# Head of a Fourier-mixing and routed-expert kernel: the second batch's first stage by way of DRAM

## The chip, the cores and the metric

The kernel runs on one core of a Trainium2 chip. The metric is the device time of one execution in microseconds (us). An engine executes its own instructions strictly in the order in which the program gave them to it, so an instruction that waits holds back everything behind it on that engine. PE is TensorE (matmuls and transposes), DVE VectorE, ACT ScalarE, POOL GpSimd, SP SyncE, which here only starts transfers. ACT and POOL start transfers too, in line with their other work.

## The reference, cut to what matters

```python
x: (8, 2496, 256) f32; filt_r, filt_i: (1249, 256); token_ids: (19968,)
w1: (8, 256, 1024); w2: (8, 1024, 256)

X = np.fft.rfft(x, axis=1)
y = np.fft.irfft(X * (filt_r + 1j * filt_i)[None], n=2496, axis=1)
x = y.reshape(19968, 256)
expert = token_ids * 2654435761 % 8
for e in range(8):
    h = np.maximum(x[expert == e] @ w1[e], 0)
    out[expert == e] = h @ w2[e]
```

## The kernel before, in words

**Mixing, per batch.** The transform over 2496 = 39 x 64 positions is done as two nested small transforms, each a matmul against a table, all in fp32. Stage 1 (table `wf_t`) makes 20 complex bins of the 39-point transform for each of 64 sequences. Stage 2 takes two bins at a time: `forward` multiplies by the table `d_t`, DVE multiplies the result in PSUM by the filter (`y`, two halves `z`, and their sum: four instructions), and `back_c` or `back` multiplies by the table `e_t`. Stage 3 (table `wi_t`) ends the inverse transform. Stage 1 and stage 3 are cut into six pieces u of four columns (the last has two), stage 2 into ten pieces.

**Two ways between the stages.** Between stages 1 and 2, and between 2 and 3, the partition axis changes. Batches 2 to 7 do that through DRAM: `stage1` stores to `d1`, `load2` reads it back, `back` stores to `d2`, `load4` reads. Batches 0 and 1 (`first` and `second`) stay on chip: `stage1_c` leaves channels on partitions in `mixed`, `turn2` transposes them for stage 2 with PE and a copy by ACT, `back_c` leaves channels on partitions again in `self.out`, and `turn4` transposes for stage 3 (copies by ACT for batch 0, by DVE for batch 1).

**Scatter and tiles.** `stage3` writes the rows and the number of each token into a buffer `o` (the number by one small DVE instruction, L401; the rows by ACT copies, L259 and L254), and POOL scatters each column with an indirect DMA (L414) into the list `xs`, sorted by expert. One batch has 22 such scatters. Then come 80 expert tiles of 256 tokens (`step`, later `late_step`). Tiles of a stage hold tokens of certain batches only: the first ones those of batches 0 and 1, so their rows (`load`, L807) are fetched when the 44th scatter has landed. The remaining batches are mixed between the tiles' matmuls.

**The head** is everything ahead of the first tile. Its order is a hand-written list `todo` of pairs (t, piece), sorted by t; t is only an order. The order of before: stage 1 of `first`; then a chain of twenty steps for both batches with stage 1 of `second` between them; `turn4` and `stage3` of `first` from the eighth chain step on; then those of `second`; stage 1 of batch 2 between and behind them; `begin`, `load` of tiles 0 and 1. `way_back` makes `e_t` on chip from `d_t` in five pieces. `weights(i, which)` starts the weight transfers of tile i, on ACT's queue for the first two tiles. `begin` opens the tiles' memory pools where the routing pool, the second pair of `o` buffers (`o2`) and others lay, and makes the sums of the first tile's weights (`weight_sums`, L840) on DVE; those of the second follow on POOL.

**Memory that is used twice.** `wts` is both the weights of two tiles and, earlier, input rows and batch 0's `out`. `mid` holds the first batch's `mixed` in rows 0 to 4 and later the slots `t2` and `t1`; the second's data lie in rows 5 to 9.

Of the kernel before, what the change touches and what calls it, by code (L numbers as in the profile page):

```python
# [11 lines left out]
F32 = mybir.dt.float32  # L12
I32 = mybir.dt.int32
# [6 lines left out]
P = 128  # L20
# [14 lines left out]
SG = 4  # L35
# [65 lines left out]
            d.transpose(1, 0, 2, 3, 4).reshape(P, NS, P).astype(f32))  # L101


def route_table():


    t = np.zeros((P, 2 * G + 1 + NQP + HN + 1), np.float32)
    p = np.arange(P)
    r = np.arange(NR)
    t[:NR, G + 1 + NQP:G + 1 + NQP + HN + 1] = (N2 * (r % N1) + np.array(H0)[r // N1])[:, None] + np.arange(HN + 1)  # L110
    for g, b in enumerate(STAGES):
        t[:, g] = p < b * S // NJ
        t[:, G + 1 + NQP + HN + 1 + g] = t[:, g] - (t[:, g - 1] if g else 0)
    t[:, G] = sum(stage_tiles(), []) + [NT] * (P - NT)
    t[:, G + 1:G + 1 + NQP] = p[:, None] * NQP + np.arange(NQP)
    return t
# [3 lines left out]
def kernel(  # L120
# [12 lines left out]
    wf_dram = nc.inline_tensor(wf_host, name="wf_tbl")  # L133
    wi_dram = nc.inline_tensor(wi_host, name="wi_tbl")
    d_dram = nc.inline_tensor(d_host, name="d_tbl")
    r_dram = nc.inline_tensor(route_table(), name="r_tbl")

    xs = nc.dram_tensor("xs", (NT * TB, W), F32)
# [73 lines left out]
    class Batch:  # L212


        def __init__(self, b):
            self.b = b
            self.d1 = self.d2 = None
            self.x, self.t2, self.t4, self.p = {}, {}, {}, {}
            self.g = None
            if b < 2:  # L220

                own = mid[:, 5 * b:5 * b + 5, :].rearrange("p k f -> p (k f)")
                self.mixed = own.rearrange("p (h n s) -> p h n s", h=2, s=NS)
                after = (held[:, 0:NS * C] if b == 0 else mid[:, 0:5, :].rearrange("p k f -> p (k f)"))
                self.out = after.rearrange("p (h n s) -> p h n s", h=2, s=NS)

        def load1(self, v):

            k = self.b * NV + v if self.b < 2 else NV + NV * (self.b > 2) + v
            if k <= NV:  # L230
                xt = wts[0:NR, k, :].rearrange("p (j c) -> p j c", c=C)
            else:
                xt = xpool.tile([NR, XL, C], F32, name=f"x_{self.b}_{v}", tag="x")
            self.x[v] = xt

            n = min(XL, HN + 1 - XL * v)
            for h in range(H):

                (nc.scalar if self.b == 0 and h == 1 else nc.sync).dma_start(out=xt[h:NR:H, 0:n, :],
                                  in_=bass.AP(tensor=x.tensor, offset=x.offset + (self.b * S + H0[h] + XL * v) * C,  # L240
                                              ap=[[N2 * C, N1], [C, n], [1, C]]))
# [28 lines left out]
        def stage1(self, u):  # L270
            if self.d1 is None:
                self.d1 = dpool.tile([N2, 2 * NS, C], F32, name=f"d1_{self.b}", tag="d1")
            v, half = divmod(u, XL // XG)
            sl = slice(half * XG, half * XG + XG)
            if half == 0:
                self.t1 = slot("t1")
            self.products(wf_t, (NR, NR), 2 * NS, self.x[v][:, sl, :], self.t1[:, sl, :], nc.scalar.copy, u, "pa")
            if half == 1:


                moves = self.parts(self.d1, self.t1, v)
                if self.b == 2 and v > 0:
                    put_off.extend(moves)
                    return
                for dram, chip in moves:
                    nc.scalar.dma_start(out=dram, in_=chip)
# [9 lines left out]
        def forward(self, u):  # L296
            ps = fps.tile([P, 2, C], F32, name=f"pb_{self.b}_{u}", tag="f")
            for i in range(2):
                s = 2 * u + i
                rhs = self.t2[u][:, i, :] if self.b < 2 else self.t2[s // SG][:, s % SG, :]  # L300
                nc.tensor.matmul(out=ps[:, i, :], lhsT=d_t[:, s, :], rhs=rhs, start=True, stop=True)  # L301


# [32 lines left out]
        def stage1_c(self, u):  # L336
# [2 lines left out]
            cols = 2 * NS * (H * n if XG * u + n <= HN else H * (n - 1) + 1)  # L339
            c0 = XG * u * 2 * NS * H  # L340
            for h in range(2):
                ps, tag = (fps, "f") if self.b == 0 else (banks["ad"[h]], "ad"[h])
                ps = ps.tile([P, 4, P], F32, name=f"pa_{self.b}_{u}_{h}", tag=tag)
                flat = ps[:].rearrange("p a b -> p (a b)")
                for i in range(n):
                    a = 2 * NS * H * i
# [25 lines left out]
        def turn4(self, u):  # L372
# [2 lines left out]
                self.t4[v] = t4pool.tile([NK, XL, C], F32, name=f"t4_{self.b}_{v}", tag="t4")  # L375
            copy = nc.vector.tensor_copy if self.b else nc.scalar.copy
            for k in range(0, min(XG, HN + 1 - XG * u), 2):
                ps = banks["ad"[k // 2]].tile([P, 2, C], F32, name=f"pu_{self.b}_{u}_{k}", tag="ad"[k // 2])
                rows = [2 * NS * (H if XG * u + k + i < HN else 1) for i in range(2)]
                for i in range(2):  # L380
                    n0 = 2 * H * (XG * u + k + i)
# [15 lines left out]
        def stage3(self, u):  # L397

            n = min(XG, HN + 1 - XG * u)
            o = (o2pool if self.b < 2 and u % 2 else opool).tile([NR, XG, W], F32, name=f"o_{self.b}_{u}", tag="o")  # L400
            nc.vector.tensor_scalar(o[:, 0:n, C:].bitcast(I32),  # L401
                                    tokno[:, XG * u:XG * u + n].unsqueeze(2).to_broadcast([NR, n, W - C]),
                                    float(self.b * S), None, op0=OP.add)
            v, half = divmod(u, XL // XG)
# [22 lines left out]
    def weights(i, which):  # L427
# [2 lines left out]
            return  # L430
        if i >= 2 and which == 0:
            ws[i] = ws[i - 2][0:2]
        eng, kw = nc.scalar if i < 2 else nc.sync, {}
        if which == 0:
            ws[i].append(eng.value_load(chunk_i[0:1, 0, i:i + 1], min_val=0, max_val=E - 1))
            if i >= 2:
# [16 lines left out]

    rctx = ctx.enter_context(ExitStack())
    rpool = pool(rctx, "route", 1)
    o2pool = pool(rctx, "o2", 2)
    nc.sync.dma_start(out=wf_t[:], in_=wf_dram.ap())
    tok_h = dataclasses.replace(moe_token_ids.tensor, shape=list(moe_token_ids.tensor.shape))
    tok = rpool.tile([P, NJ, 2], I32)
# [265 lines left out]
    def chain(k):  # L725

        for step, j in ((Batch.turn2, k + 1), (Batch.back_c, k - 2), (Batch.forward, k)):
            if 0 <= j < NS:
                step(batches[j // (NS // 2)], j % (NS // 2))


    def warm(n):

# [1 line left out]
        for k in range(n):  # L735
            nc.tensor.matmul(out=ps[:, k % 4, :], lhsT=ident[:], rhs=ident[:], start=True, stop=True)

    todo = [(-165, lambda: warm(14))]
    todo += [(t, lambda k=k: load_tables(k)) for k, t in enumerate((-160, -159, -157, -156))]
    todo += [(t, lambda v=v: second.load1(v)) for v, t in enumerate((-159.5, -156.5, -156.4))]  # L740
    todo += [(t, lambda u=u: first.stage1_c(u)) for u, t in enumerate(spaced(-155, -151, NU))]
    todo += [(-154.2, count), (-152, route), (-150.9, later)]
    todo += [(-137.2, places), (-128, tile_experts), (-121, experts), (-90, blanks)]
    todo += [(t, lambda k=k: pads(k)) for k, t in enumerate((10.9, 11.6, 11.9, 16.9, 17.6, 17.95, 22.9))]
    todo += [(t, lambda k=k: spread_filters(k)) for k, t in enumerate((-150.45, -146.6, -143, -137.6))]
    todo += [(t, lambda k=k: way_back(k)) for k, t in enumerate((-150.44, -146.5, -141.8, -137.5, -133.8))]
    todo += [(-150.4, lambda: first.turn2(0))]
    todo += [(t, lambda k=k: chain(k)) for k, t in enumerate(spaced(-150, -105, NS + 2))]
    todo += [(t, lambda u=u: second.stage1_c(u)) for u, t in enumerate(spaced(-147.5, -132, NU))]
    for bt, at in ((first, spaced(-123.7, -105, NU)), (second, spaced(-103, -85, NU))):  # L750
        todo += [(t - 2.6, lambda bt=bt, u=u: bt.turn4(u)) for u, t in enumerate(at)]
        todo += [(t, lambda bt=bt, u=u: bt.stage3(u)) for u, t in enumerate(at)]
    todo += [(-135, lambda: nc.sync.dma_start(out=wi_t[:], in_=wi_dram.ap()))]
    todo += [(t, lambda v=v: batches[2].load1(v)) for v, t in enumerate((-119, -117.5, -116))]
    todo += [(t, lambda u=u: batches[2].stage1(u)) for u, t in enumerate((-101.5, -99.5, -84.8, -84.7, -84.6, -84.5))]

    todo += [(-75.5, lambda: [nc.sync.dma_start(out=dram, in_=chip) for dram, chip in put_off])]
    todo += [(t, lambda k=k: weights(k // 2, k % 2)) for k, t in enumerate((-101, -98, -95, -92))]
    todo += [(-84.9, lambda: begin()), (-84.4, lambda: [load(i) for i in range(2)])]

    def batch(b, t1, t2, t3):

# [5 lines left out]
            out += part1(b, a1, [max(x0, a1[2 * v] - 2.5) for v in range(NV)])  # L768
        return out

    todo += [(-75 + .1 * g, lambda g=g: batches[2].load2(g)) for g in range(4)]
    todo += [(-74.5 + .1 * v, lambda v=v: batches[3].load1(v)) for v in range(2)]
    todo += part2(2, spaced(1, 3.5, N_2), [None] * 4 + [1.5], .6)
    todo += part3(2, spaced(4.6, 7.5, NU), [4.0, 4.1, 4.8]) + part1(3, spaced(1, 4, NU), [None, None, 2])
    todo += part2(3, spaced(6.4, 10, N_2), [5.2, 5.4, 5.6, 6.5, 7.5], .6)
# [15 lines left out]
    def begin():  # L791
        nonlocal gath, work, outs, nums, tpool
        rctx.close()
        tpool, nums, gath = pool(ctx, "tp", 2), pool(ctx, "nums", 8), pool(ctx, "gath", 2)
        outs, work = pool(ctx, "outs", 2), pool(ctx, "work", 1)
        weight_sums(0, nc.vector)

# [36 lines left out]
    def weight_sums(i, eng=None):  # L834

        eng, w1, h = eng or nc.gpsimd, ws[i][0], F // 2
        b11, b12, b21, b22 = [w1[:, d, f * h:f * h + h] for d in range(DP) for f in range(2)]
        t = [tpool.tile([P, h], F32, name=f"tw_{i}_{k}", tag=f"tw{k}") for k in range(4)]
        for k, (p, q) in enumerate(((b12, b11), (b22, t[0][:]), (b22, b12), (b21, t[1][:]))):
            eng.tensor_tensor(t[k][:], p, q, op=OP.subtract)  # L840
        sums[i] = t
# [252 lines left out]
```

## Time and profile before

| | us |
|---|---|
| median of 3 runs | 1433.88 (1428.81 to 1435.61) |
| the profiled execution | 1467.31 |
| its span | 1465.5 |
| first scatter (POOL L414) starts | 74.27 |
| the 44th scatter of the head starts | 144.71 |
| first matmul of the first tile (L850) | 153.56 |

All times on the trace's axis are from the start of the span of the profiled execution. The head is the part before 153.56 us. A row of the timeline has the start, the duration, the engine, the line and the names, and in brackets the idle time ahead of it and what ended it. A row of the windows has, for each engine, busy us and the number of instructions, then PE's granted clock, the share of the DMA engines and GB/s.

### The profile page before, as it was taken

The numbers are of one execution on the slowest core, as the hardware profiler recorded it, in microseconds if no ns is written. First come the engines' busy times: TensorE is split into PE (matmuls) and PEld (weight loads), VectorE is DVE, ScalarE is ACT, GpSimd is POOL, SyncE is SP. The second block draws the span as 40 slices with busy tenths as digits, with TensorE's granted clock in tenths as the row PEclk, the third lists the DMA queues.
The fourth block names the chain that finished last, engine by engine and source line by source line (L and its number), as shares of the span: only waits on it lengthen the run. The fifth ranks groups of instructions, "written<-read, shape, count | busy, mean of one in ns | idle before, by whom it ended". The sixth has DMA issues, their size and how long they took to land.

```text
span 1465.5 us, 26476 instructions
## 1 busy us (share of the span) xinstructions
PE 1397.5 (95%) x9494; PEld 1296.0 (88%) x9494; DVE 877.6 (60%) x1641; ACT 419.1 (29%) x770; POOL 822.0 (56%) x732
## 2 busy tenths in 40 slices
PE   8988799899999989999999999999999999999997
PEld 8876688788988878888999899998999999999997
DVE  7862565366465546533666367744557767677765
ACT  4543122223223212322222222222222222222222
POOL 5065332763475464558435387878955555555553
PEclk9998799999999999999999999999999999999999
DMA  8236775767887597797764777688661616161611
GB/s 231 77 101 214 184 218 158 207 200 238 261 258 252 154 295 234 221 281 227 229 199 139 202 215 235 201 244 247 194 216 44 210 44 208 44 215 45 212 45 34
DMA packets 240947, 272.32 MB, mean 186 GB/s; under 512 B 124940, under 2 KB 210879, under 8 KB 231389
## 3 DMA queue, kind: packets, MB, share of 16 engines
q1 hardware_dynamic: 89087, 169.76, 37.3%
q10 hardware_dynamic: 131806, 56.23, 15.8%
q0 software_dynamic: 19920, 44.59, 8.7%
q8 instruction: 78, 1.28, 0.4%
q14 instruction: 56, 0.46, 0.1%
HBM read 290.24 MB, written 83.53 MB: 255 GB/s over the span
## 4 chain that ended last, share of the span: by engine, by line
PE 78%; DMA 10%; DVE 4%; issue 3%; another core or an unknown queue 1%; POOL 1%; ACTq 1%; ACT 1%; SPq 0%; POOLq 0%; DVEq 0%
PE dps L885 18%; PE up_b L850 8%; PE up_a L850 5%; PE up_c L850 5%; PE pd L257 4%; PE pb L301 4%; PE dnc L912 4%; PE dnb L912 4%; PE dna L912 4%; PE upc L907 4%; PE upa L907 4%; PE pc L324 3%; PE pa L257 2%; DMA t<-d 2%; PE upe L907 2%
## 5 line engine op out<-in xcount | busy, mean ns | idle before, releaser
L885 PE MATMUL dps<-wts,ht 128*128 128x256 f32 x1600 | 367.8, 380 | 1.3 <-ACT ht L854 1.3
L885 PEld LDWEIGHTS dps<-wts,ht 128*128 128x128 f32 x1600 | 302.5, 190 | 45.1 <-ACT ht L854 1.9
L977 POOL DMA_INDIRECT out_dram<-osb,no x158 | 165.1, 1045 | 228.3 <-DVE osb L919 142.8
L414 POOL DMA_INDIRECT xs<-o,sidx x176 | 176.1, 1000 | 197.0 <-ACT o L259 73.4
L840 POOL TENSOR_TENSOR tw<-wts 128x512 f32<-128x512 f32 x158 | 204.3, 1293 | 112.9 <-DMA wts<-in_moe_w_dram 86.2
L840 POOL TENSOR_TENSOR tw<-wts,tw 128x512 f32<-128x512 f32 x158 | 205.1, 1298 | 6.2
L857 DVE TENSOR_TENSOR ht<-up_b,ht 128x512 f32<-128x512 f32 x150 | 103.7, 691 | 141.6 <-PE up_b L850 79.9
L854 ACT ACTIVATE ht<-ht 128x512 f32<-128x512 f32 x150 | 94.3, 630 | 205.7 <-DVE ht L857 172.7
L850 PE MATMUL up_a<-xt,wts 128*128 128x128 f32 x800 | 118.8, 283 | 22.4 <-ACT ht L861 12.8
L850 PEld LDWEIGHTS up_a<-xt,wts 128*128 128x128 f32 x800 | 108.7, 198 | 26.8 <-ACT ht L861 14.1
L311 DVE TENSOR_TENSOR z<-pb,filt 64x512 f32<-64x512 f32 x160 | 110.2, 689 | 36.8 <-PE pc L324 33.4
L890 DVE COPY osb<-dps 128x512 f32<-128x512 f32 x50 | 34.6, 692 | 161.0 <-PE dps L885 112.0
L850 PE MATMUL up_b<-st,tw 128*128 128x128 f32 x800 | 110.9, 284 | 5.8 <-DVE ht L857 4.6
L850 PEld LDWEIGHTS up_b<-st,tw 128*128 128x128 f32 x800 | 101.5, 199 | 7.8 <-issue 7.5
L857 DVE TENSOR_TENSOR ht<-up_c,ht 128x512 f32<-128x512 f32 x100 | 69.0, 690 | 42.9 <-PE up_c L850 29.7
L916 ACT ACTIVATE ht<-ht 128x512 f32<-128x512 f32 x90 | 56.8, 631 | 120.6 <-DVE ht L919 75.2
L257 PE MATMUL pd<-t,wi_t 120*117 120x256 f32 x320 | 79.1, 390 | 7.8 <-DVE t L387 4.0
L327 ACT COPY mid<-pc 128x512 f32<-128x512 f32 x60 | 35.0, 583 | 151.5 <-PE pc L324 94.6
L307 DVE TENSOR_TENSOR y<-pb,filt 128x512 f32<-128x512 f32 x80 | 55.2, 690 | 37.7 <-PE pb L301 25.0
L861 ACT COPY ht<-up_a 128x512 f32<-128x512 f32 x50 | 29.3, 586 | 165.3 <-PE up_a L850 98.2
L257 PEld LDWEIGHTS pd<-t,wi_t 120*117 120x117 f32 x320 | 58.1, 186 | 20.4 <-issue 4.2
L259 ACT COPY o<-pd 117x512 f32<-117x512 f32 x80 | 44.4, 585 | 107.5 <-PE pd L257 40.3
(210 smaller groups left out, 2507.6 us busy)
## 6 DMA issues: line engine op xcount, KB each, us to landing
wts<-in_moe_w_dram SPq DMA_DIRECT2D x160, 1024.0 KB
xg<-xs ACTq DMA_DIRECT2D x321, 64.0 KB
mid<-d SPq DMA_DIRECT2D x60, 256.0 KB
d<-mid ACTq DMA_DIRECT2D x60, 256.0 KB
d_t<-t2s SPq DMA_DIRECT2D x15, 1024.0 KB
e_t<-t2s SPq DMA_DIRECT2D x15, 1024.0 KB
t<-d SPq DMA_DIRECT2D x12, 960.0 KB
x<-in_x_dram SPq DMA_DIRECT2D x36, 312.0 KB
```

The costliest lines, as they stand in the source:

```text
L257: nc.tensor.matmul(out=ps[0:cols * H, k, :], lhsT=w[:], rhs=src[:, 2 * i + k, :], start=True, stop=True)
L301: nc.tensor.matmul(out=ps[:, i, :], lhsT=d_t[:, s, :], rhs=rhs, start=True, stop=True)
L311: nc.vector.tensor_tensor(out=z[b], in0=ps[a], in1=f_t[1][64 * hi:64 * hi + 64, s1:s1 + 2, :], op=OP.mult)
L414: st = nc.gpsimd.indirect_dma_start(out=xs[:], out_offset=bass.IndirectOffsetOnAxis(ap=index, axis=0), in_=rows, in_offset=None, bounds_ch ...
L840: eng.tensor_tensor(t[k][:], p, q, op=OP.subtract)
L850: nc.tensor.matmul(out=ps[bank][:, f, :], lhsT=w[:, f * P:(f + 1) * P], rhs=xx, start=first and f == 0, stop=True, skip_group_check=True)
L854: nc.scalar.activation(out=out, in_=in_, func=AF.Relu)
L857: nc.vector.tensor_tensor(out, ps[bank][:], other, op=OP.add)
L885: nc.tensor.matmul(out=ps[:, h, :], lhsT=ht[:, h, fp, :], rhs=w2[:, fp, :], start=(fp == 0), stop=(fp == FP - 1))
L907: nc.tensor.matmul(out=ps[:, f, :], lhsT=w[:, f * P:(f + 1) * P], rhs=xx, start=first and f == 0, stop=True, skip_group_check=True)
L912: nc.tensor.matmul(out=ps[:, 0, :], lhsT=a[:, f, :], rhs=b[:, f, :], start=first and f == 0, stop=True, skip_group_check=True)
L977: st = nc.gpsimd.indirect_dma_start(out=out[:], out_offset=bass.IndirectOffsetOnAxis(ap=to_rows[i][:, h:h + 1], axis=0), in_=o[:, h, :], i ...
```

## The change

- `second` runs `stage1` (through `d1` in DRAM and `load2`) in place of `stage1_c` and `turn2`; its stages 2 and 3 stay on chip, `out` now in rows 5 to 9 of `mid`.
- `way_back` makes 8 of the 20 parts of `e_t`; the other 12 come from a new DRAM table `e_tbl` by an SP transfer.
- Batch 2 gets a third input buffer (`x2`) and no longer uses a row of `wts`; its stage-1 results go to rows 0 to 3 of `mid`.
- The first two tiles' weights are started by SP.
- The token-number instruction of `stage3` goes to POOL for batches 0 and 1; `turn4` of batch 1 takes the PSUM banks b and c for its odd pieces, a and d for the even ones.
- The two buffers of the weight sums become two pools of one buffer each.
- The head's order list is written anew.

```diff
+def back_table(d):
+    e = d.transpose(2, 1, 0).copy()
+    e[0:64] *= -1
+    return e[:, 8:].copy()
...
+    e_dram = nc.inline_tensor(back_table(d_host), name="e_tbl")
...
-                own = mid[:, 5 * b:5 * b + 5, :].rearrange("p k f -> p (k f)")
-                self.mixed = own.rearrange("p (h n s) -> p h n s", h=2, s=NS)
-                after = (held[:, 0:NS * C] if b == 0 else mid[:, 0:5, :].rearrange("p k f -> p (k f)"))
+                if b == 0:
+                    own = mid[:, 0:5, :].rearrange("p k f -> p (k f)")
+                    self.mixed = own.rearrange("p (h n s) -> p h n s", h=2, s=NS)
+                after = (held[:, 0:NS * C] if b == 0 else mid[:, 5:10, :].rearrange("p k f -> p (k f)"))
...
-            if k <= NV:
+            if self.b == 2 and v == 2:
+                xt = x2pool.tile([NR, XL, C], F32, name="x_2_2", tag="x")
+            elif k <= NV and self.b < 2:
...
-                self.t1 = slot("t1")
+                self.t1 = (slot("t1") if self.b != 2 else
+                           mid[0:NK, 2 * (v % 2):2 * (v % 2) + 2, :].rearrange("p k (j c) -> p (k j) c", c=C))
...
-                rhs = self.t2[u][:, i, :] if self.b < 2 else self.t2[s // SG][:, s % SG, :]
+                rhs = self.t2[u][:, i, :] if self.b == 0 else self.t2[s // SG][:, s % SG, :]
...
-                ps, tag = (fps, "f") if self.b == 0 else (banks["ad"[h]], "ad"[h])
-                ps = ps.tile([P, 4, P], F32, name=f"pa_{self.b}_{u}_{h}", tag=tag)
+                ps = fps.tile([P, 4, P], F32, name=f"pa_{self.b}_{u}_{h}", tag="f")
...
-                ps = banks["ad"[k // 2]].tile([P, 2, C], F32, name=f"pu_{self.b}_{u}_{k}", tag="ad"[k // 2])
+                tag = ("bc" if self.b and u % 2 else "ad")[k // 2]
+                ps = banks[tag].tile([P, 2, C], F32, name=f"pu_{self.b}_{u}_{k}", tag=tag)
...
-            nc.vector.tensor_scalar(o[:, 0:n, C:].bitcast(I32),
+            (nc.gpsimd if self.b < 2 else nc.vector).tensor_scalar(o[:, 0:n, C:].bitcast(I32),
...
-        eng, kw = nc.scalar if i < 2 else nc.sync, {}
+        eng, kw = nc.sync, {}
...
-    o2pool = pool(rctx, "o2", 2)
+    o2pool, x2pool = pool(rctx, "o2", 2), pool(rctx, "x2", 1)
...
-            if 0 <= j < NS:
-                step(batches[j // (NS // 2)], j % (NS // 2))
+            if 0 <= j < N_2:
+                step(first, j)
...
+    head += [(t, lambda u=u: first.stage1_c(u)) for u, t in enumerate(spaced(10, 14, NU))]
...
+    head += [(t, lambda k=k: spread_filters(k)) for k, t in enumerate((22.8, 29, 35.3, 44.8))]
+    head += [(t, lambda k=k: way_back(k)) for k, t in enumerate((22.9, 29.1))]
+    head += [(22.95, lambda: first.turn2(0))]
+    head += [(23 + 3.6 * k, lambda k=k: chain(k)) for k in range(N_2 + 2)]
+    head += [(30, lambda: nc.sync.dma_start(out=e_t[:, 8:, :], in_=e_dram.ap()))]
+    head += [(30.1, lambda: nc.sync.dma_start(out=wi_t[:], in_=wi_dram.ap()))]
+    head += [(t, lambda u=u: second.stage1(u)) for u, t in enumerate((27, 32, 38, 41, 45, 48.5))]
+    head += [(41.5, places), (64, tile_experts), (70, experts), (118, blanks)]
+    head += [(t, lambda g=g: second.load2(g)) for g, t in enumerate((54, 54.1, 54.2, 54.3, 70))]
+    head += [(61 + 2.9 * u, lambda u=u: second.forward(u)) for u in range(N_2)]
+    head += [(61 + 2.9 * (u + 2) - .1, lambda u=u: second.back_c(u)) for u in range(N_2)]
+    at = (64, 69, 74, 79.5, 85, 90)
+    head += [(t, lambda u=u: first.turn4(u)) for u, t in enumerate(at)]
+    head += [(t + 3, lambda u=u: first.stage3(u)) for u, t in enumerate(at)]
+    head += [(t, lambda v=v: third.load1(v)) for v, t in enumerate((72, 73, 74))]
+    head += [(t, lambda k=k: weights(k // 2, k % 2)) for k, t in enumerate((95, 95.1, 95.2, 95.3))]
+    head += [(96 + 5 * u - 4 * (u > 0), lambda u=u: second.turn4(u)) for u in range(NU)]
+    head += [(98 + 5 * u, lambda u=u: second.stage3(u)) for u in range(NU)]
+    head += [(99 + 5 * u - 3 * (u == 5), lambda u=u: third.stage1(u)) for u in range(NU)]
+    head += [(123.5, lambda: begin()), (123.6, lambda: [load(i) for i in range(2)])]
+    head += [(124, lambda: [nc.sync.dma_start(out=dram, in_=chip) for dram, chip in put_off])]
...
+    todo = [(t - 200, piece) for t, piece in head]
...
-        tpool, nums, gath = pool(ctx, "tp", 2), pool(ctx, "nums", 8), pool(ctx, "gath", 2)
+        tpool, nums, gath = [pool(ctx, f"tp{k}", 1) for k in range(2)], pool(ctx, "nums", 8), pool(ctx, "gath", 2)
...
-        t = [tpool.tile([P, h], F32, name=f"tw_{i}_{k}", tag=f"tw{k}") for k in range(4)]
+        t = [tpool[i % 2].tile([P, h], F32, name=f"tw_{i}_{k}", tag=f"tw{k}") for k in range(4)]
```

More of the change, by code (lines that the diff above doesn't have):

```diff
@@ L736, in warm @@
             nc.tensor.matmul(out=ps[:, k % 4, :], lhsT=ident[:], rhs=ident[:], start=True, stop=True)
[L738 to L743, printed above, removed]
@@ L744 @@
-    todo += [(t, lambda k=k: pads(k)) for k, t in enumerate((10.9, 11.6, 11.9, 16.9, 17.6, 17.95, 22.9))]
[L745 to L755, printed above, removed]
@@ L757 @@
-    todo += [(-75.5, lambda: [nc.sync.dma_start(out=dram, in_=chip) for dram, chip in put_off])]
-    todo += [(t, lambda k=k: weights(k // 2, k % 2)) for k, t in enumerate((-101, -98, -95, -92))]
-    todo += [(-84.9, lambda: begin()), (-84.4, lambda: [load(i) for i in range(2)])]
+    third = batches[2]
+    head = [(0, lambda: warm(14))]
+    head += [(t, lambda k=k: load_tables(k)) for k, t in enumerate((5, 6, 8, 9))]
+    head += [(t, lambda v=v: second.load1(v)) for v, t in enumerate((5.5, 8.5, 8.6))]
@@ new lines @@
+    head += [(t, lambda u=u: first.stage1_c(u)) for u, t in enumerate(spaced(10, 14, NU))]
+    head += [(10.8, count), (13, route), (14.1, later)]
+    head += [(t, lambda k=k: spread_filters(k)) for k, t in enumerate((22.8, 29, 35.3, 44.8))]
[3 more added lines that the diff above has]
+    head += [(30, lambda: nc.sync.dma_start(out=e_t[:, 8:, :], in_=e_dram.ap()))]
@@ new lines @@
+    head += [(99 + 5 * u - 3 * (u == 5), lambda u=u: third.stage1(u)) for u in range(NU)]
+    head += [(123.5, lambda: begin()), (123.6, lambda: [load(i) for i in range(2)])]
+    head += [(124, lambda: [nc.sync.dma_start(out=dram, in_=chip) for dram, chip in put_off])]
+    head += [(125 + .1 * g, lambda g=g: third.load2(g)) for g in range(4)]
+    head += [(125.5 + .1 * v, lambda v=v: batches[3].load1(v)) for v in range(2)]
+    todo = [(t - 200, piece) for t, piece in head]
+    todo += [(t, lambda k=k: pads(k)) for k, t in enumerate((10.9, 11.6, 11.9, 16.9, 17.6, 17.95, 22.9))]
@@ L769, in batch @@
         return out
-    todo += [(-75 + .1 * g, lambda g=g: batches[2].load2(g)) for g in range(4)]
-    todo += [(-74.5 + .1 * v, lambda v=v: batches[3].load1(v)) for v in range(2)]
     todo += part2(2, spaced(1, 3.5, N_2), [None] * 4 + [1.5], .6)
```

## The prediction, written before the changed kernel was seen

> **What bounds the kernel now.** I read the page first, then the busy time by stretches of the head, the list of waits from 55 us on, and last the timeline around the longest waits. The page says that the span is PE's.
>
> ```profile
> PE 1397.5 (95%) x9494; PEld 1296.0 (88%) x9494; DVE 877.6 (60%) x1641; ACT 419.1 (29%) x770; POOL 822.0 (56%) x732
> ```
>
> That holds for the tiles, which the change leaves alone. Only the head can get shorter, and it has four stretches with limits of their own, then a gap ahead of the first tile.
>
> ```profile
> 0.00:24.00 24.00, 20.09 (x132) 19.79 (x132) 15.92 (x59) 8.44 (x15) 8.10 (x22) 0.93 0.84 222
> 24.00:64.00 40.00, 37.16 (x266) 35.03 (x266) 35.01 (x48) 21.78 (x38) 13.88 (x13) 1.00 0.44 110
> 64.00:102.40 38.40, 36.60 (x235) 32.29 (x235) 30.37 (x62) 22.70 (x40) 16.75 (x17) 1.00 0.38 118
> 102.40:145.60 43.20, 34.00 (x140) 25.22 (x140) 10.04 (x28) 13.89 (x27) 27.17 (x28) 0.80 0.63 197
> 145.60:153.60 8.00, 0.04 (x1) 0.04 (x1) 6.34 (x6) 0.00 (x0) 6.26 (x5) 0.61 0.61 114
> ```
>
> The reader is to see: input transfers in the first; PE and DVE nearly full in the second; PE (36.6 of 38.4) in the third; no engine full in the fourth, at a granted clock of 0.80; PE idle in the last. The end of the fourth is POOL's last scatter, and how POOL got there is in the waits and the timeline:
>
> ```profile
> POOL xs L414 <- DVE o L401: 14.6, 2, 14.2
> ...
> DVE tw L840 <- DMA xs<-o,sidx: 10.5, 1, 10.5
> ...
> 74.27 1.09 POOL L414 DMA_INDIRECT xs<-o,sidx  x1 [14.25 <-DVE o L401]
> ...
> 96.88 0.99 POOL L414 DMA_INDIRECT xs<-o,sidx  x1 [5.09 <-ACT mid L370]
> ...
> 124.34 5.77 ACTq L445 DMA_DIRECT2D wts<-in_moe_w_dram  x2
> ...
> 128.46 0.99 POOL L414 DMA_INDIRECT xs<-o,sidx  x1 [0.30 <-issue]
> 130.29 0.58 ACT L259 COPY o<-pd 117x512 f32<-117x512 f32 x1 [6.97 <-DMA xs<-o,sidx]
> 131.17 0.99 POOL L414 DMA_INDIRECT xs<-o,sidx  x1 [1.72 <-issue]
> ...
> 144.71 0.90 POOL L414 DMA_INDIRECT xs<-o,sidx  x1 [0.30 <-issue]
> ...
> 152.81 0.70 DVE L818 STREAM_TRANSPOSE xt<-xg 128x512 f32<-128x512 f32 x1
> ```
>
> A scatter costs POOL 0.99 us and 0.30 ahead of it. 44 x 1.29 = 56.8 us, but 74.27 to 145.61 is 71.3, so POOL stood for 14.6 us. The largest pieces: 4.8 at 91.8, about 2.2 each near 110 and 117, about 4 from 128.5 to 135.7. The last has a plain cause: ACT's copies into `o` stood behind a weight transfer that took ACT's queue 5.77 us to start.
>
> **The change part by part.** Every duration is from the profiled execution (1467.31 us; the median run, 1433.88, is 0.977 of it).
>
> *Start, 0 to 24 us:* the same pieces in the same order; nothing.
>
> *24 to 63 us.* PE: a piece of `stage1` is 8 instructions in 1.73 us, of `stage1_c` 16 in 1.78; equal. Three `way_back` pieces go, 0.44 us of PE and 0.69 of ACT each. DVE ends this stretch (the tenth filter product ends at 63.8); its work is the same, but `places` moves forward and can fill DVE's hole of 1.33 us before 48.64, so the products end at 62.5. Against that, `stage1` takes two of the four shared PSUM buffers that `stage1_c` left alone, so PE may wait for DVE; I book the two at 0 to +2. The new table transfer is 0.79 MB on SP behind all input; at the 242 to 247 GB/s of 25 to 40 us it takes 3.1 us, and since the DMA engines are 0.97 busy until 40 and 0.31 after, it lands near 45. Its first user, `back_c`(4), ran at 46.7: hidden, by a margin of 2 us; if late, PE pays it.
>
> *The round trip.* The last `stage1` piece ends on ACT near 54. The nearest row for a store that is read again is `slots`: POOL waited 1.8 us behind its issue. Store 0.64 MB: 2.6 + 1.8; load of the first group, 0.52 MB: 2.1 + 1.8; together 8.3, landing at 62.3. The Trainium skill ("DMA: Bandwidth & Descriptors", Anatomy of one DMA) gives 2.0 us per transfer plus bytes over 436 GB/s, warning of long completion when DRAM is written: 3.5 + 3.2 = 6.7, landing at 60.7. The row is dearer, and I take it. Either way the cover is DVE's backlog until 62.5. `load2` has to wait too for the last `turn2`, near 55, which reads the same rows of `mid`.
>
> *The middle.* Ten `turn2` of `second` go: 10 x 0.64 = 6.4 us of PE, 10 x 0.59 of ACT. PE's work from the second's first `forward` to the first's last `stage3`: 10 x (0.87 + 0.89) + 4.8 (`turn4`) + 9.6 (`stage3`) + 0.3 = 32.3, so 63 to about 96; DVE needs 10 x 2.85 + 2.4 = 31, close behind. In the order list 5.3 us of PE work stand between the first `forward` and `stage3`(0), then 1.7 until ACT has half an `o`: first scatter at 70.5 in place of 74.27. Before, that half was ready at 70.8, and POOL waited for L401 behind DVE's products.
>
> *L401 on POOL.* 12 instructions of 117 x 16 join POOL's own chain. POOL runs none before. The GpSimd rows of like size are 0.20 (copy of one element), 0.29 (128 x 128 select); on DVE it took 0.17. The skill ("GPSIMD Engine Reference", Engine selection) speaks against the move: elementwise work belongs on VectorE, with GpSimd about twice as slow on two inputs and near line rate on one. Twice 0.17 is 0.34. I take 0.3, 3.6 us in all; ends 0.1 and 0.6 (1.2 and 7.2 us). It waits for the scatters of four pieces earlier, with 16 scatters (20 us) between, against 3.5 us that the last scatter took to land; queued behind it are that piece's scatters.
>
> *The scatter chain.* Supply: PE's second part is 5 x (0.87 + 1.73 + 1.73) + 2.4 = 24 us, from 96 to about 121; a piece comes each 4.3 us or, in the middle, 5.2, and POOL needs 5.5. So POOL is never out of work for long and becomes the limit: 70.5 + 56.8 + 3.6 + 2.5 for pauses = 133.4. The 2.5 is my choice: half of the 4.8 at 91.8, which followed two pauses of ACT (2.3 and 2.2 us, ended by nothing recent), whose like may come again.
>
> *Weights on SP.* Six transfers leave ACT's queue (1.5 + 0.5 + 5.8 + 0.6 us of its time). SP starts nothing between 73 and 145, so its 8.4 us from about 96 delay nothing else; `load`, `put_off` and `load2` behind them come 20 us later. 4.2 MB at 250 GB/s land by 114, and the third input buffer frees row 3 of `wts` for them.
>
> *The gap.* The rows of tile 0 landed near 150.2, but DVE got to their transpose only at 152.81, since its weight sums waited 10.5 us for scatters out of `o2`, whose memory they take over, and then ran beside POOL's. As a separate pool of 8 KB the first sums lie where routing data lay, about 13 KB, and run earlier: -2.55. The gap shrinks from 7.95 to 5.4.
>
> *The sum.* First tile at 133.4 + 5.4 = 138.8 against 153.56: -14.8. Everything after moves along. 1467.31 - 14.8 = 1452.5 profiled; 14.8 x 0.977 = 14.5 off the median: 1419.4.
>
> **The rivals.**
> - *POOL stands again (gain 4 to 11).* ACT's pauses return while POOL has no backlog, 4.8 us each, or L401 costs 0.6, or the new PSUM sharing delays the chain. For: the row at 96.88. Against: a backlog builds from the second batch on. Two pauses: 14.8 - 7.1 = 7.7 off the profiled time, 1426.4.
> - *Everything fits (gain 18 to 22).* First scatter at 69, L401 at 0.1, no pause: 69 + 56.8 + 1.2 + 5.4 = 132.4, so -21.2 profiled, 1413.2. PE then ends near 121, so POOL alone decides.
> - *The round trip comes too late (slower).* `second.forward`(0) stands in PE's queue ahead of all `turn4` and `stage3`, so every us past 62.5 moves the first scatter. It decides from a landing at about 77 on, and costs over 0.5% from 85: landing at 87 gives +9.7, 1443.4. For: near 151 a store to `d1` and its `load2` lie 10.5 us apart. Against: there SP was held by the gathers of tokens; here the DMA engines move 0 to 22 GB/s from 45 to 65 us.
> - *It doesn't act.* If POOL's stand comes from something that the order doesn't touch, the gain is the 2.55 of the gap and little else: 1430.
>
> **How the numbers follow.** Chances: the sum with gains of 11 to 18, 0.58; everything fits, 0.15; POOL stands again, 0.20, of which 0.15 above 7.2 us; no action, 0.02; the late round trip, 0.05. A measurement of this kernel can tell 0.5%, 7.2 us, from no change: faster 0.58 + 0.15 + 0.15 = 0.88; same 0.05 + 0.02 = 0.07; slower 0.05. The range holds the sum, most of the two neighbours and 2 us for the spread of the runs (1428.8 to 1435.6): 1411 to 1428.
>
> **What would show it.** Right: scatters at 1.29 us with hardly a gap from 70 to 133, with a POOL instruction of about 0.3 us each fourth; `load2` landed before DVE is done with batch 0; ACT's queue free of weights; PE done ahead of POOL; DVE's weight sums before the rows land; the first L850 near 139. Wrong: PE idle near 62 to 70 waiting for `mid<-d`; POOL gaps that end with ACT or DVE; L850 before 133 or after 146; or tiles of a different length than before.

## The result, and the profile after

| us | before | after |
|---|---|---|
| median (lowest to highest), same chip | 1430.75 (1426.38 to 1438.34) | 1426.28 (1421.33 to 1433.15) |
| the profiled execution | 1467.31 | 1421.33 |
| first scatter starts | 74.27 | 71.56 |
| last scatter of the head ends | 145.61 | 134.90 |
| first matmul of the first tile | 153.56 | 140.52 |

The ratio is 0.9955, with a 95% interval of 0.9941 to 0.9969. Of 1430.75 us that is 6.4 us, between 4.4 and 8.4; the medians lie 4.5 apart. Here and below, runs that lie over 1.5% above the lowest of the same kernel are left out of medians and ratios. The kernel became faster, but by about the 0.5% that the prediction called what can be told from no change, and by less than half of the forecast 14.5.

The two profiled executions give another picture: their spans differ by 46 us, and the first tile begins 13.0 us earlier. Which of the two figures belongs to the change is the question of the experiments.

The profile after, first its busy line:

```profile
PE 1368.2 (96%) x9398; PEld 1271.0 (90%) x9398; DVE 897.2 (63%) x1629; ACT 412.6 (29%) x757; POOL 830.2 (58%) x744
```

Then the windows of the head, with the columns of those of before:

```profile
24.00:64.00 40.00, 35.20 (x202) 30.62 (x202) 34.88 (x48) 18.04 (x31) 13.80 (x14) 0.99 0.78 220
64.00:102.00 38.00, 37.83 (x238) 32.80 (x237) 31.15 (x59) 20.75 (x37) 24.25 (x26) 0.97 0.68 225
102.00:130.00 28.00, 20.16 (x106) 16.06 (x104) 9.18 (x22) 11.82 (x23) 21.57 (x26) 0.90 0.61 193
130.00:145.00 15.00, 4.48 (x21) 4.48 (x22) 3.33 (x6) 0.59 (x1) 8.90 (x9) 0.50 0.55 127
```

From 64 to 102 us PE is full. From 102 on it has work for 20 of 28 us, and POOL's 21.6 busy us together with the 0.30 ahead of each scatter leave no hole. The waits from 55 to 145 us (engine, line, what it waited for: sum, times, longest; "issue" is a wait for nothing that the profile shows) say so:

```profile
POOL xs L425 <- ACT o L269: 16.5, 3, 15.9
POOL xs L425 <- issue: 7.9, 26, 0.3
POOL xs L425 <- POOL o L412: 3.3, 11, 0.3
PE pb L312 <- DMA mid<-d: 2.4, 1, 2.4
```

The timeline has the steps one by one:

```profile
61.90 1.10 PE L312 MATMUL pb<-mid,d_t 128*128 128x256 f32 x4 [2.44 <-DMA mid<-d]
...
71.56 1.14 POOL L425 DMA_INDIRECT xs<-o,sidx  x1 [15.86 <-ACT o L269]
...
82.66 0.69 DVE L323 TENSOR_TENSOR y<-y,z 128x512 f32<-128x512 f32 x1
82.66 0.80 POOL L412 TENSOR_SCALAR o<-tokno 117x16 int32<-117x16 f32 x1
...
103.74 0.25 POOL L412 TENSOR_SCALAR o<-tokno 117x16 int32<-117x16 f32 x1
...
119.65 0.69 DVE L857 TENSOR_TENSOR tw<-wts 128x512 f32<-128x512 f32 x1
...
133.99 0.91 POOL L425 DMA_INDIRECT xs<-o,sidx  x1 [0.30 <-issue]
...
139.75 0.71 DVE L835 STREAM_TRANSPOSE xt<-xg 128x512 f32<-128x512 f32 x1 [17.48 <-DMA xg<-xs]
140.52 1.86 PE L867 MATMUL up_a<-xt,wts 128*128 128x128 f32 x7 [18.36 <-DVE xt L835]
```

After its first scatter POOL never waits for over 0.31 us. The chain from 71.56 to 134.90 is 44 scatters (44.8), 0.30 ahead of 43 of them (12.9), and 5.6 for the 11 token-number instructions that lie within it, of which 4.9 are their durations and the rest small spaces around them. PE reads the second batch's rows at 61.90, after a wait of 2.44 for the round trip. DVE sums the first tile's weights at 119.65, long before the rows are there.

### The profile page after: what moved, and what is told of

Read it like the earlier page. It is cut to its first block, busy times and chain, and to the rows that moved or that the text cites. A ratio compares the mean times of both kernels' runs of the same rounds, so it can differ in the third digit from the quotient of the medians.

```text
span 1419.6 us, 26284 instructions
## 1 busy us (share of the span) xinstructions
PE 1368.2 (96%) x9398; PEld 1271.0 (90%) x9398; DVE 897.2 (63%) x1629; ACT 412.6 (29%) x757; POOL 830.2 (58%) x744
## 4 chain that ended last, share of the span: by engine, by line
PE 81%; DMA 9%; DVE 3%; issue 3%; POOL 2%; ACT 1%; ACTq 1%; SPq 1%; POOLq 0%; DVEq 0%
PE dps L902 21%; PE up_b L867 8%; PE up_a L867 5%; PE up_c L867 5%; PE pd L267 4%; PE pb L312 4%; PE dnc L929 4%; PE dna L929 4%; PE dnb L929 4%; PE upc L924 4%; PE upa L924 4%; PE pa L267 3%; PE pc L335 3%; PE upe L924 2%; PE upg L924 2%
## 5 line engine op out<-in xcount | busy, mean ns | idle before, releaser
L857 POOL TENSOR_TENSOR tw<-wts 128x512 f32<-128x512 f32 x158 | 205.1, 1298 | 112.2 <-DMA wts<-in_moe_w_dram 84.7
L857 POOL TENSOR_TENSOR tw<-wts,tw 128x512 f32<-128x512 f32 x158 | 204.5, 1294 | 6.2
L267 PE MATMUL pd<-t,wi_t 120*117 120x256 f32 x320 | 75.9, 379 | 2.2 <-DMA t<-d 2.2
L312 PE MATMUL pb<-mid,d_t 128*128 128x256 f32 x280 | 73.5, 385 | 2.8 <-DMA mid<-d 2.4
L323 DVE TENSOR_TENSOR y<-y,z 128x512 f32<-128x512 f32 x80 | 71.4, 892 | 2.7
```

Of the source, the lines that this page charges most:

```text
L267: nc.tensor.matmul(out=ps[0:cols * H, k, :], lhsT=w[:], rhs=src[:, 2 * i + k, :], start=True, stop=True)
```

## The experiments

Two readings of the small gain stood against each other. In the first, the head gains the forecast 14 us and the tiles give most of it back (theory A). In the second, the head itself gains less than its record says. To separate them, the head is timed alone: every tile but the first, and what follows the tiles, is left out of both kernels.

```diff
-    for i in range(NSURE):
...
-        step(i)
...
-    rest(0)
-    store(NSURE - 1, (1, 0))
+    step(0)
+    store(0)
```

**Both kernels and both heads, on one chip.**

> The unchanged kernel of before, profiled once more, because its first profiled execution (1467.31 us) lay 36 us above its median. Theory A (the head's gain of 13.0 us between the two first profiles is real, and 8 to 9 us of it are lost in the tiles): first tile again at 152 to 155 us, tiles about 1275 us long instead of 1312. Theory B (the first profile was slow in the head as well, and the real gain of the head is about 5 us): first tile at 144 to 147 us, tiles about 1283 us.

> The changed kernel, profiled once more and timed in five rounds. Both theories: first tile at 139 to 142 us and a ratio of 0.993 to 0.998. Theory A: tiles of 1280 to 1287 us in an execution near the median, 5 to 10 us longer than those of the kernel before; theory B: tiles of the same length as before within 3 us.

> The kernel of before with its head and the first tile alone; the other tiles and the last blocks are left out. It times the head without the tiles. First tile at 153 us by theory A, 145 by theory B; end of the execution some 20 us later.

> The changed kernel with its head and the first tile alone; the other tiles and the last blocks are left out. Theory A: 12 to 14 us shorter than the head of before in the timed runs; theory B: 4 to 7 us shorter.

On this chip the kernel before took 1466.08 us (median, 1457.6 to 1473.4), not 1430.75, and the one after 1457.20: ratio 0.9943 (0.9922 to 0.9963), or 8.4 us. The heads took 183.49 and 178.30. As parts of the whole kernel before they are 0.1254 (0.1246 to 0.1262) and 0.1218 (0.1211 to 0.1226), a difference of 5.3 us. So the head's gain and the whole kernel's agree within their intervals, and theory A, which expected 12 to 14 us of the heads, falls; theory B had 4 to 7.

The two whole profiles met neither theory. Their first tiles stand at 158.32 (before) and 148.41 (after), and those of the heads alone at 158.14 and 150.57, later than either expected. What follows in the whole profiles takes 1298.2 and 1318.2 us. But the execution of before lies 8 us below its median and that of after 11 us above, so their difference says nothing of the tiles.

The level is the surprise: 1466 is where the profiled execution of before lay (1467.31), while that of after lay at the other chip's level. The profiled executions of this chip have spans of 1456.5 us (before) and 1466.6 (after), those of the two records 1465.5 and 1419.6. The 46 us between the two records are therefore for the most part not the change, but two levels of the same work. That the record of before came from a chip of the upper level is inferred from its time, and from pauses of ACT that agree within 0.02 us with those of this chip's profile (last section).

**The heads on a chip of the lower level** (whole kernel before: 1432.77).

> The head and the first tile of before once more (the other tiles and the last blocks are left out), to be compared with e6 in the same five rounds. Whether the head's gain depends on the chip: if this chip runs the whole kernel of before in about 1430 us and the gain of the head was overrated from a slow chip's profile, its first tile comes at 145 to 149 us here; if the head takes as long everywhere, at 153 to 158.

> The changed head and the first tile (the rest left out). If the whole gain of the change is the head's: shorter than e5 by what the whole kernel gains, 4 to 8 us; if tiles give something back, by 10 us or more.

178.36 against 172.31: 6.1 us. As parts of the whole kernel before they are 0.1248 (0.1242 to 0.1254) and 0.1207 (0.1201 to 0.1213), a difference of 0.0041, or 5.9 us. Within the intervals, the gain of the whole kernel (6.4, 4.4 to 8.4) is all here. The timeline of the old head at this level:

```profile
74.58 1.10 POOL L414 DMA_INDIRECT xs<-o,sidx  x1 [14.30 <-DVE o L401]
...
93.56 0.99 POOL L414 DMA_INDIRECT xs<-o,sidx  x1 [1.45 <-ACT t L387]
...
117.86 4.43 ACTq L445 DMA_DIRECT2D wts<-in_moe_w_dram  x2
122.46 0.59 ACT L259 COPY o<-pd 117x512 f32<-117x512 f32 x1 [5.55 <-PE pu L383]
125.78 1.00 POOL L414 DMA_INDIRECT xs<-o,sidx  x1 [1.26 <-DMA xs<-o,sidx]
...
136.91 0.90 POOL L414 DMA_INDIRECT xs<-o,sidx  x1 [0.30 <-issue]
...
145.74 2.08 PE L850 MATMUL up_a<-xt,wts 128*128 128x128 f32 x8 [11.32 <-DVE xt L818]
```

And of the new head:

```profile
71.12 1.14 POOL L425 DMA_INDIRECT xs<-o,sidx  x1 [14.73 <-ACT o L269]
...
132.91 0.92 POOL L425 DMA_INDIRECT xs<-o,sidx  x1 [0.30 <-issue]
...
139.60 2.08 PE L867 MATMUL up_a<-xt,wts 128*128 128x128 f32 x8 [17.17 <-DVE xt L835]
```

The old head starts its scatters as late as in the record (74.58), but ends them at 137.81 in place of 145.61: POOL stood for 6.0 us in it, not for 14.4. Of these 8.3 us, 3.6 are missing from the stop ahead of the scatter at 96.88 in the record (5.09, here 1.45 at 93.56), 3.0 from the two near 110 and 117, and 1.6 from those behind the weight transfer. Ahead of the first, ACT paused twice in the record:

```profile
90.29 0.58 ACT L361 COPY wts<-pt 128x512 f32<-128x512 f32 x1 [2.30 <-PE pb L301]
...
93.10 0.69 ACT L370 COPY mid<-pc 128x512 f32<-128x512 f32 x1 [2.22 <-PE pt L357]
```

At the same two instructions of the old head here both pauses are missing:

```profile
88.13 0.59 ACT L361 COPY wts<-pt 128x512 f32<-128x512 f32 x1
88.97 0.69 ACT L370 COPY mid<-pc 128x512 f32<-128x512 f32 x1 [0.25 <-PE pc L368]
```

The first tile moves from 145.74, where it was expected if the record had overrated the gain, to 139.60, by 6.1 us. There is no trace of the whole kernel before at this level; of the new kernel there is, and its first tile (140.52) lies within 0.9 us of that of its head alone.

**Single parts of the new head, same chip.** The token numbers back on DVE:

```diff
-            (nc.gpsimd if self.b < 2 else nc.vector).tensor_scalar(
+            nc.vector.tensor_scalar(
```

> The changed head and the first tile, with the token-number instruction of stage 3 back on VectorE. If POOL's scatter chain is the limit of the new head: 12 instructions of 0.25 us and 0.30 us ahead of each leave it, 4 to 7 us shorter than e6. If the supply by PE and ACT is the limit: within 1 us of e6. If VectorE's queue delays the numbers as before: 2 to 4 us longer.

As parts of the whole kernel before, 0.1203 (0.1199 to 0.1208) against 0.1207 (0.1201 to 0.1213): the two aren't told apart, and the 4 to 7 us of a pure POOL limit didn't come. The traces show two effects against each other. POOL's chain becomes 4.2 us shorter (58.5 against 62.7), but begins 1.8 us later, since the first number now stands behind DVE's filter products:

```profile
71.85 0.17 DVE L412 TENSOR_SCALAR o<-tokno 117x16 int32<-117x16 f32 x1
...
72.92 1.10 POOL L425 DMA_INDIRECT xs<-o,sidx  x1 [17.76 <-DVE o L412]
```

Its first tile stands at 137.24, 2.4 us earlier than in the other trace, but that is one execution of each. Moving the numbers to POOL gains nothing that these runs resolve.

The weights of the first two tiles back on ACT's queue:

```diff
-        eng, kw = nc.sync, {}
+        eng, kw = nc.scalar if i < 2 else nc.sync, {}
```

> The changed head and the first tile, with the first two tiles' weights started by ScalarE again. If POOL has a backlog that covers ACT's stand of up to 8 us: 0 to 2 us longer than e6. If ACT's copies feed POOL without reserve: 4 to 8 us longer.

176.15 against 172.31. As parts, 0.1231 (0.1224 to 0.1238) against 0.1207 (0.1201 to 0.1213): 3.4 us longer, between the two cases expected. In the traces the first tile comes 2.9 us later (142.48). The timeline shows the price where the prediction had looked for it:

```profile
99.02 1.44 ACTq L456 DMA_DIRECT2D wts<-in_moe_w_dram  x2
...
101.92 2.28 ACTq L456 DMA_DIRECT2D wts<-in_moe_w_dram  x2
...
105.39 1.07 ACT L269 COPY o<-pd 117x512 f32<-117x512 f32 x2 [6.77 <-DMA wts<-in_moe_w_dram]
...
106.79 1.05 POOL L425 DMA_INDIRECT xs<-o,sidx  x1 [2.62 <-issue]
```

ACT's copies into `o` stand for 6.77 us behind the transfers, and POOL for 2.62 behind them. The unchanged new head pauses for 2.20 us at the same copy, so the transfers add about 4.6.

**The same part in the old head, and the split pool.** These ran on a chip where the kernel before took 1467.22. The old head with nothing but its weights moved to SP:

```diff
-        eng, kw = nc.scalar if i < 2 else nc.sync, {}
+        eng, kw = nc.sync, {}
```

The new head with one pool of two buffers for the weight sums:

```diff
-        tpool, ... = [pool(ctx, f"tp{k}", 1) for k in range(2)], ...
+        tpool, ... = pool(ctx, "tp", 2), ...
-        t = [tpool[i % 2].tile(...) for k in range(4)]
+        t = [tpool.tile(...) for k in range(4)]
```

> The changed head and the first tile (the rest left out), as the measure for e10 and e11 on the same chip: about 172.7 us where the whole kernel of before takes about 1432, about 178.5 where it takes about 1466.

> The head of before and the first tile (the rest left out), with one part of the change alone: the first two tiles' weights started by SyncE. If moving them is what the change gains (taking it back cost 4.2 us): within 2 us of e9, that is 4 to 6 us shorter than the head of before. If the old head has other limits beside it, the stands of POOL before 122 us: 1 to 3 us shorter than the head of before, 3 to 5 us longer than e9.

> The changed head and the first tile (the rest left out), with the weight sums' buffers in one pool of two as before. If the first sums then wait again for the scatters out of the second pair of buffers and hold up the transpose of the first tile: 1.5 to 2.6 us longer than e9. If the first tile's rows land late enough to cover them: within 0.7 us.

The new head took 178.96, or 0.1218 (0.1211 to 0.1225) of the whole kernel, the same part as on the other chip of this level. The old head with its weights on SP took 187.38, or 0.1275 (0.1268 to 0.1283); the old head as it was had 0.1254 (0.1246 to 0.1262) on that other chip. So this part, worth 3.4 us in the new order, costs about 3 us in the old one, where 1 to 6 us less had been expected. The two old heads were timed on different chips, and their traces don't show the cost: the first tile stands at 157.82 with the weights on SP and at 158.14 without. What the timeline shows is one longer stop:

```profile
104.60 2.49 SPq L445 DMA_DIRECT2D wts<-in_moe_w_dram  x2
...
113.50 0.69 ACT L370 COPY mid<-pc 128x512 f32<-128x512 f32 x1 [5.72 <-remote]
114.24 1.96 PE L383 MATMUL pu<-ident,mid 128*120 128x128 f32 x8 [7.95 <-ACT mid L370]
```

ACT did nothing for 5.72 us while the weights came in, and PE stood for 7.95 behind it. At the same instruction of the unchanged old head ACT paused for 2.25. No event in the trace ends this pause ("remote"); that the weights make it longer isn't shown.

The single pool's time gives no verdict: five of its six runs took 182.8 to 183.8 us, over 1.5% above the sixth, 179.19, which is as long as the two pools took. What the single pool does is plain in the trace: DVE's weight sums wait again, and the transposed rows come late. First the single pool's DVE rows, then the two pools':

```profile
144.76 0.69 DVE L857 TENSOR_TENSOR tw<-wts 128x512 f32<-128x512 f32 x1 [14.99 <-DMA xs<-o,sidx]
...
150.38 0.70 DVE L835 STREAM_TRANSPOSE xt<-xg 128x512 f32<-128x512 f32 x1
```

```profile
147.00 0.71 DVE L835 STREAM_TRANSPOSE xt<-xg 128x512 f32<-128x512 f32 x1 [14.76 <-DMA xg<-xs]
```

From the end of the last scatter to the first tile it is 7.95 us with one pool (143.18 to 151.13) and 5.52 with two (142.25 to 147.77). All eight traces with two pools have 5.5 to 5.8 us here, and the five of the old head, with its one pool, 7.9 or more.

**A version that tries to take both advantages**: the whole kernel after, with POOL making the first number only (so that the chain begins early) and DVE all others.

```diff
-            (nc.gpsimd if self.b < 2 else nc.vector).tensor_scalar(
+            (nc.gpsimd if self.b == 0 and u == 0 else nc.vector).tensor_scalar(
```

> The whole changed kernel, with the token numbers written by VectorE except for the first piece of batch 0, which POOL, idle then, writes. POOL's chain loses 11 of 12 instructions (0.25 us, and 0.30 ahead of each) and keeps its early start: first tile 2 to 5 us earlier than the changed kernel's (139.6 to 140.5 us on a fast chip), ratio to before 0.991 to 0.995; if VectorE's queue delays the numbers instead, ratio 0.995 to 0.998.

1457.42 us, ratio to before 0.9938 (0.9915 to 0.9961). The kernel after had 0.9943 (0.9922 to 0.9963) on another chip of this level. The two aren't told apart. Its first tile stands at 142.43, against 148.41, but this profile is the shortest of its kernel's runs and the other the longest.

The round trip through DRAM, the table from DRAM, the third input buffer, the PSUM banks and the new order weren't undone one by one. What each of them gives or costs isn't shown.

## Why the prediction was right in its place and wrong in its size

The median, 1426.28, lies in the range of 1411 to 1428, but near its end, and the forecast was 6.9 us too low. The gain of 6.4 us is within the 7.2 that the text itself called no change, a case to which it gave 0.07. The steps, taken at the level of the median (the heads on the chip at 1432.77):

| step | predicted | measured |
|---|---|---|
| second batch's rows landed | 62.3 | PE reads them at 62.68 (record: 61.90) |
| first scatter | 70.5 | 71.12 (71.56) |
| 44 scatters | 56.8 | 57.6 (57.7) |
| token numbers on POOL, with the spaces around them | 3.6 | 3.8 (5.6) |
| POOL's stops | 2.5 | 1.3 (0) |
| last scatter ends | 133.4 | 133.83 (134.90) |
| gap to the first tile | 5.4 | 5.77 (5.62) |
| first tile, after | 138.8 | 139.60 (140.52) |
| first tile, before | 153.56 | 145.74 |

**The changed head came out as predicted**, at the lower level, each step within some 2.5 us and the sum within 0.8 to 1.7.

- *Round trip.* The store was issued by 53.97 and the rows were used at 61.90, 7.9 us later. The prediction had 8.3 from the `slots` row, and 6.7 as an estimate from the Trainium skill's rule ("DMA: Bandwidth & Descriptors", Anatomy of one DMA). That rule is fitted to transfers that GpSimd starts, and here ACT started the store and SP the load; the row was the better measure. The cover was thinner than thought: DVE's backlog ended at 61.04, not at 62.5, and DVE then stood for 2.00. The first scatter's delay of 0.6 to 1.1 us may come from there; that isn't shown.
- *Other supply.* PE first used `e_t` at 45.66, after a wait of 0.35 for it (predicted: landed near 45), and was done with the head at 122.2 (about 121).
- *Token numbers.* Alone they take 0.25 us. Of the 11 that lie within the chain of the record, four took 0.76 to 0.80. Each of these began within 0.05 us of a DVE instruction that reads two inputs from SBUF (`y<-y,z`, L323, or `tw<-wts,tw`, L857) and ended 0.11 to 0.12 us after it: the one at 82.66 ends at 83.46, and DVE's, which began at the same time and took 0.69, at 83.35. The Trainium skill ("SBUF — State Buffer", SBUF: two separate sides) has the rule: such a DVE instruction and a GpSimd one that reads SBUF exclude each other for a whole instruction. The times agree with it; no run was made to test it. The prediction weighed only the rule on speed and left this one out. The four took 2.1 us more together than at 0.25 each, about the excess over 3.6.
- *Weights on SP, the pools.* Both were given a cause in the trace, and undoing each brings that cause back: 3.4 us for the queue by time, and for the pools 2.4 us of gap (predicted 2.55) by the trace alone.

**What failed is the first term of the subtraction**: "first tile at 133.4 + 5.4 = 138.8 against 153.56", and with it "14.8 x 0.977 = 14.5 off the median". The profiled execution of before was 33 us above the median run, and the prediction took that as a stretch of 2.3% that lies evenly over all of it. It doesn't. At the level of the median the old head's first tile is at 145.74, so 7.8 of those us lie in its first tenth, and they lie in POOL's stops that the change was to remove. With that baseline the same sum gives 145.74 - 138.8 = 6.9, and the measurement was 6.1 by the traces, 5.9 by the heads' parts and 6.4 by the whole kernel's ratio.

At the upper level, from which 153.56 and all durations of the sum came, the other side fails. There the whole new kernel's first tile stands at 148.41, not at 138.8: the first scatter starts at 72.47, 2.0 us late, and POOL stands for 8.9 us where the sum booked 2.5. The sum set an old head with the stops of one level against a new one nearly without them. That 138.8 fits the lower level is in part luck, and so is it that the median lies in the range, 1.7 us from its upper end.

The warning was there to see: the profiled execution, at 1467.31, lay outside all three runs shown. And the stops that ended with ACT's pauses, "ended by nothing recent", carried no cause that the change could remove. The prediction said so of their return in the new head, but not of their absence from the old one.

The rival "POOL stands again" names the time measured, 1426.4, but at this level not by its mechanism: POOL stands for 0 to 1.3 us in the new head. At the upper level its mechanism is seen, with 7.8 to 8.9 us of stops in the new head, and the gain is 5.3 (head) to 8.4 us (whole) all the same, since the old one stands for 13 to 14. Of "The round trip comes too late" and "It doesn't act" nothing is seen.

Three slips of the working don't bear on this: 71.3 less 56.8 is 14.5, not 14.6; POOL's stops from 128.5 to 135.7 are 3.3 us when counted like the others, not about 4; and 0.79 MB at the rate named take 3.2 us, not 3.1.

## What to carry to other kernels

Before a stall is counted as a gain, compare the profiled execution's time with the timed runs. Where it lies outside them, the excess need not be spread evenly (here 7.8 of 33 us lay in the first tenth), and a stop without a releaser is the first place to look for it: such a stop may be missing from the runs that count. A part taken alone can change its sign with the order around it (weights on SP: 3.4 us gained in one order, about 3 lost in the other), so a part is undone in the new kernel as well as done in the old. And a head can be timed alone when a few us of 1430 are the question.

## What was not expected of the hardware

**Two levels.** The same kernel took 1430.75 and 1432.77 us in two sets of runs, and 1466.08 and 1467.22 in two others, on other chips: about 2.4% apart. Each chip was used at one time only. In the timed runs the mean granted clock was 0.984 to 0.992 at the lower level and 0.975 to 0.987 at the upper. The new kernel's whole profile at the upper level has this busy line:

```profile
PE 1387.9 (95%) x9398; PEld 1282.5 (87%) x9398; DVE 869.6 (59%) x1629; ACT 411.3 (28%) x757; POOL 827.7 (56%) x744
```

Against the record of after, PE is busy for 19.7 us longer and the span is 47.0 us longer; the other engines are no busier. So less than half of the difference lies in PE's own instructions, and where the rest comes from is open.

**Pauses that recur at the same instruction.** On ACT, the first copy of the second batch in the new head follows a pause of 2.17 to 2.20 us in three traces of the lower level, and of 5.07 to 5.12 in four of the upper. First two rows of the lower level (the record of after, the new head alone), then two of the upper (the whole kernel after, the new head alone). The releaser named isn't the same in all:

```profile
100.67 0.59 ACT L269 COPY o<-pd 117x512 f32<-117x512 f32 x1 [2.20 <-issue]
```

```profile
100.94 0.58 ACT L269 COPY o<-pd 117x512 f32<-117x512 f32 x1 [2.20 <-POOL o L412]
```

```profile
109.17 1.07 ACT L269 COPY o<-pd 117x512 f32<-117x512 f32 x2 [5.07 <-POOL o L412]
```

```profile
108.59 1.07 ACT L269 COPY o<-pd 117x512 f32<-117x512 f32 x2 [5.11 <-POOL o L412]
```

The old head has the like: 2.30, 2.22, 2.23 and 5.04 us at four instructions of ACT in the record of before, and 2.29, 2.22, 2.23 and 5.05 at the same four in the other whole run of the upper level. In the old head's trace at the lower level the first three are missing, and the fourth is 2.72. So the pauses belong to the place in the program and to the level.

What they are stays open. The traces have a few packets of instruction fetch, and one of them lies inside most of these pauses: at 100.02 and 100.55 us in the two of 2.20, at 105.25 and 104.53 in those of 5.07 and 5.11, and in the old head at 109.50 in the 5.04 and at 105.08 in the 2.72. None lies inside the record's pauses of 2.30, 2.22 and 2.23. No run was made to move a fetch, so that fetches cause the pauses isn't shown.
